# Up-projection of six of twelve hidden chunks in the last two token tiles by Strassen's seven block products

## The chip, the cores and the metric

The kernel runs on one core of a Trainium2 chip. The metric is device time in microseconds of one launch; before the change it is 357.53 us (median of three runs, 356.72 to 358.25). The profiled execution used below took 358.99 us by the same clock, of which its trace covers 357.2 us from the first to the last instruction. Engines are called as in the profile: PE (matrix multiply), PEld (its weight loads), DVE (vector), ACT (scalar), POOL (GpSimd), SP (the queue that issues most transfers).

## The reference

The program is blockwise causal attention followed by a gated feed-forward layer.

```python
scores = scale * np.matmul(q, k.transpose(0, 1, 3, 2))   # (8, 8, 576, 64) per q, k, v; blocks of 64
... masked softmax over scores -> attn ...
x = np.matmul(attn, v).transpose(0, 2, 1, 3).reshape(4608, 512)
gate = np.maximum(x @ w_gate, 0.0)        # w_gate: 512 x 1536
val = x @ w_val                            # w_val:  512 x 1536
out = (gate * val) @ w_out                 # w_out:  1536 x 512
```

Inputs and the output are float32; inside the kernel the matrix products take bf16 and accumulate in float32.

## The kernel before, in words

**Tiles.** The 4608 tokens are handled as nine tiles of 512: tiles j = 0 to 7 hold the first 512 tokens of batch j, tile 8 holds the 64 last tokens of all eight batches. `xT_of(j)` is the transposed attention output of tile j, 128 partitions by four contraction chunks c by 512 tokens; for tile 8 it is `xTt`. The feed-forward of tile j runs while the attention of batch j + 1 runs in between its matmuls, so while tiles 7 and 8 run no attention is left.

**Up-projection.** The 1536 hidden features are twelve chunks f of 128. For every chunk `product` (L866) issues four matmuls of 128 x 512 for the gate and four for the value, one per contraction chunk c. ACT takes the relu of the gate out of the PSUM bank (`relu`, L876) and DVE multiplies it with the value's bank into the hidden tile `hT` (`hidden`, L886). The banks come from the pool `ffnp`, a ring of three; there are also two double banks `sc`, used by the attention, and one bank `one`.

**Down-projection.** From tile 2 on (`SEVEN = 2`) `seven_products` forms the output by Strassen's scheme over the blocks (chunk parity) x (token half) and (chunk parity) x (output half): seven sums of products instead of eight, each of 12 matmuls of 128 x 256 (L789), whose left sides are sums of hidden blocks. The pairs of chunks (2c, 2c + 1) are numbered c = 0 to 5. `Sums.make_part` (L748) makes the left sides on DVE: part 0 for the products 5 and 2, part 1 for product 1, part 2 for the products 6 and 7. The order of the products is 5 into the bank `y` and 2 into the bank `z` (first for c = 0 to 3, then for c = 4, 5), then 1, 3, 4, 6, 7. ACT, DVE and POOL combine the banks in float32 tiles `ob` (a ring of four; L823 to L846), which transfers on the ACT queue then write out; one store is kept back and issued in the next tile.

**Order.** Every engine executes its instructions in the order in which the program issues them. `ffn_gen` is a generator that yields after a few matmuls; the attention's steps carry a place in that sequence of yields (`AT`), and a loop at the end of the kernel issues each step when the generator has come to its place.

Of the kernel before, what the change touches and what calls it, by code (L numbers as in the profile page):

```python
# [10 lines left out]
FP = mybir.dt.float32  # L11
BF = mybir.dt.bfloat16
AX = mybir.AluOpType
# [4 lines left out]
def kernel(  # L18
# [10 lines left out]
    nc = tc.nc  # L29
# [9 lines left out]
    FIRST = 3  # L39
    SEVEN = 2  # L40
    BASE = {0: 0, 1: 512, 3: 896, 2: 1024}
    AW = 1600
# [64 lines left out]
    def new_bf():  # L107
        return [sb.tile([128, 2048], BF, name=n, bufs=2) for n in ("q_bf", "k_bf")]
# [593 lines left out]
    def weight_differences(c, eng):  # L702

        two = wo[c // 2][:, 2 * (c % 2) : 2 * (c % 2) + 2, :]
        for d, n in ((two[:, 0, 256:512], two[:, 1, 256:512]), (two[:, 1, 0:256], two[:, 0, 0:256])):
            eng.tensor_tensor(out=d, in0=d, in1=n, op=AX.subtract)

    class Sums:

# [21 lines left out]

        def make_part(self, q, part, k0, k1):
            h, n = self.quads[q], k1 - k0
# [10 lines left out]
            else:  # L744
                out = self.two[q][:, 1024 + 512 * k0 : 1024 + 512 * k1]
                a, b = h[:, 2 * k0 : 2 * k1, 256:512], h[:, 2 * k0 : 2 * k1, 0:256]
                op, m = AX.subtract, 2 * n
            nc.vector.tensor_tensor(  # L748
                out=out.rearrange("p (c n) -> p c n", c=m), in0=a, in1=b, op=op
# [17 lines left out]
    def seven_products(j, quads, sums):  # L767
# [30 lines left out]
        def half(to, p):  # L798
            return to[:, 256 * p : 256 * p + 256]

        def whole(to, which, new=True, cs=range(6)):
            for p in range(2):
                for c in cs:
                    times(half(to, p), which, p, c, new and (p, c) == (0, 0))
                    if c % 2:
                        yield
# [11 lines left out]
        for to, which in ((y, 5), (z, 2)):  # L818
            yield from whole(to, which, cs=range(4))
        for to, which in ((y, 5), (z, 2)):  # L820
            yield from whole(to, which, new=False, cs=(4, 5))
        g = sb.tile([128, 512], FP, name="ob", bufs=4)
# [10 lines left out]
        nc.gpsimd.tensor_tensor(out=c22, in0=g, in1=c12, op=AX.add)  # L833
        yield from whole(z, 4, new=False)
        c21 = sb.tile([128, 512], FP, name="ob", bufs=4)
        nc.scalar.copy(c21, z)
# [11 lines left out]
        else:  # L848
            for p in range(2):
# [7 lines left out]
                )  # L857
                store_later(0, 0, half(g, p), p, p + 1)

    def ffn_gen():  # L860
        for j in range(B + 1):
            hT = []
# [26 lines left out]

            sums = Sums(quads) if j >= SEVEN else None  # L890

            first = 0
# [139 lines left out]
    with tc.manual_schedule(engines={E.PE, E.DVE, E.Activation, E.Pool, E.SP}):  # L1032
# [465 lines left out]
        for b in range(4, B):  # L1498
# [17 lines left out]
            {f"D{c}": lambda c=c: weight_differences(c, nc.vector) for c in range(6)}  # L1516
        )
        for c in range(6):
            AT[f"W{c}"] = (225, 229, 233, 242, 266, 270)[c]
            AT[f"D{c}"] = 293 + 5 * c  # L1520
# [45 lines left out]
```

## Time and profile before

| what | value |
|---|---|
| median of the runs | 357.53 us |
| profiled execution | 358.99 us, span 357.2 us |
| PE busy | 346.6 us (97% of the span), 3173 matmuls |
| DVE, ACT, POOL busy | 206.2, 180.8, 143.6 us |
| PE busy between 292.9 and 352.7 us (tiles 7 and 8) | all of it |
| from PE's last matmul to the end | 4.5 us |

The profile's numbers are read so: a line of a group gives the program line (L866 is line 866 of the kernel above), the engine, the operation, its output and inputs, and the busy time with the mean duration of one instruction; the chain is the sequence of work, followed back from the last instruction, in which each step released the next; a stage's row gives each engine's busy time in that stretch and the clock that PE was granted (1.00 is full speed).

### The profile page before, as it was taken

What the parts mean: (1) busy time and instruction counts of PE and PEld (TensorE: products, weight loads), DVE (VectorE), ACT (ScalarE), POOL (GpSimd) and SP (SyncE); (2) the same over time, 40 slices, a digit from 0 to 9 for tenths busy, and PEclk for the clock granted to TensorE, in tenths of its full rate; (3) what the DMA queues carried; (4) which work ended last, traced back from release to release, by engine and by line L of the source; (5) the groups of instructions that cost most, each with busy time, mean ns of one, the idle gap of its engine ahead of it and who ended that gap; (6) DMA issues with size and microseconds to landing.
All of it is one profiled execution on the core that took longest, in us unless ns stands there. A gap on an engine that the chain in (4) does not pass through costs nothing.

```text
span 357.2 us, 8061 instructions
## 1 busy us (share of the span) xinstructions
PE 346.6 (97%) x3173; PEld 202.8 (57%) x3173; DVE 206.2 (58%) x519; ACT 180.8 (51%) x286; POOL 143.6 (40%) x187
## 2 busy tenths in 40 slices
PE   6999999999999999999999999999999999999994
PEld 3544555545444458555855576557755684485464
DVE  4654445668536675466647772667366745644661
ACT  5942756687235771566355545555465513322321
POOL 4847655589926901590149203940200020020003
PEclk9899999999999999999999999999999999999999
DMA  8999999999999995899259954999310030003004
GB/s 243 296 356 373 323 228 283 194 133 184 158 153 145 144 160 94 150 147 164 58 139 140 122 114 130 124 142 134 110 46 15 17 112 29 2 11 108 1 0 119
DMA packets 155398, 50.02 MB, mean 140 GB/s; under 512 B 134464, under 2 KB 151744, under 8 KB 155360
## 3 DMA queue, kind: packets, MB, share of 16 engines
q0 software_dynamic: 70528, 8.98, 45.2%
q1 hardware_dynamic: 76432, 31.47, 42.8%
q10 hardware_dynamic: 8400, 9.05, 7.8%
q8 instruction: 25, 0.41, 0.5%
q14 instruction: 13, 0.11, 0.1%
HBM read 37.75 MB, written 9.44 MB: 132 GB/s over the span
## 4 chain that ended last, share of the span: by engine, by line
PE 87%; DMA 4%; ACT 4%; DVE 3%; issue 0%; POOL 0%; POOLq 0%; DVEq 0%
PE ffnp L866 47%; PE ffnp L789 13%; PE one L789 5%; PE ffnp L967 3%; PE sc L451 3%; DMA kTm<-k_bf 3%; PE ffnp L586 2%; PE one L451 2%; DMA xT<-xnat 2%; PE one L586 2%; ACT attnT L456 2%; ACT attnT L415 1%; PE one L866 1%; PE one L1018 1%; PE sc L586 1%; PE ffnp L270 1%
## 5 line engine op out<-in xcount | busy, mean ns | idle before, releaser
L886 DVE TENSOR_TENSOR hT<-gate_sb,ffnp 128x512 bf16<-128x512 bf16 x102 | 69.8, 685 | 68.6 <-PE ffnp L866 44.4
L876 ACT ACTIVATE gate_sb<-ffnp 128x512 bf16<-128x512 f32 x107 | 64.4, 605 | 88.2 <-PE ffnp L866 88.0
L866 PE MATMUL ffnp<-xT,wg 128*128 128x512 bf16 x380 | 103.4, 379 | 0.8 <-DMA xT<-xnat 0.8
L866 PE MATMUL ffnp<-xT,wv 128*128 128x512 bf16 x360 | 99.0, 379 | 0.3 <-DVE hT L886 0.3
L833 POOL TENSOR_TENSOR ob<-ob 128x512 f32<-128x512 f32 x7 | 8.8, 1263 | 143.8 <-ACT ob L830 143.8
L866 PEld LDWEIGHTS <-wv 128*128 128x128 bf16 x432 | 39.6, 98 | 45.5 <-issue 5.1
L866 PEld LDWEIGHTS <-wg 128*128 128x128 bf16 x432 | 40.0, 98 | 43.0 <-issue 2.2
L456 ACT ACTIVATE attnT<-sc 128x1024 bf16<-128x1024 f32 x56 | 57.5, 1042 | 0.0
L789 PEld LDWEIGHTS <-stage 128*128 128x128 bf16 x420 | 40.3, 98 | 6.0
L748 DVE TENSOR_TENSOR stage<-hT 128x512 bf16<-128x512 bf16 (+2 forms) x84 | 38.5, 486 | 0.9
L586 PEld LDWEIGHTS <-attnT 128*128 128x128 bf16 x640 | 26.6, 98 | 12.8 <-DVE attnT L1027 1.1
L789 PE MATMUL ffnp<-stage 128*128 128x256 bf16 x252 | 31.4, 273 | 0.0
L339 POOL DMA_DIRECT2D q_bf<-in_q_dram x20 | 17.9, 908 | 24.5 <-DVE hT L886 19.0
L463 ACT ACTIVATE attnT<-one 128x512 bf16<-128x512 f32 (+1 forms) x28 | 15.0, 536 | 25.2 <-PE ffnp L451 23.5
L339 POOL DMA_DIRECT2D v_bf<-in_v_dram x30 | 24.3, 890 | 0.0
L967 PE MATMUL ffnp<-wo,hT 128*128 128x512 bf16 x96 | 23.7, 379 | 0.0
L451 PEld LDWEIGHTS <-kTm 64*128 64x128 bf16 x384 | 13.1, 94 | 14.7 <-issue 8.7
L339 POOL DMA_DIRECT2D k_bf<-in_k_dram x20 | 17.8, 931 | 0.0
L451 PE MATMUL sc<-qTm,kTm 64*128 64x512 bf16 (+1 forms) x168 | 17.7, 305 | 0.0
L789 PEld LDWEIGHTS <-hT 128*128 128x128 bf16 x168 | 16.4, 98 | 1.9
L841 DVE TENSOR_TENSOR ob<-ffnp,ob 128x512 f32<-128x512 f32 x7 | 4.8, 692 | 21.6 <-POOL ob L833 15.0
L830 ACT COPY ob<-ffnp 128x512 f32<-128x512 f32 x7 | 4.1, 586 | 21.9 <-PE ffnp L789 21.9
(144 smaller groups left out, 464.2 us busy)
## 6 DMA issues: line engine op xcount, KB each, us to landing
out_dram<-ob ACTq DMA_DIRECT2D x32, 256.0 KB, 2.4
stage<-in_moe_w_val_dram SPq DMA_DIRECT2D x6, 512.0 KB, 8.7
stage<-in_moe_w_gate_dram SPq DMA_DIRECT2D x6, 512.0 KB, 8.7
stage<-in_moe_w_out_dram SPq DMA_DIRECT2D x6, 512.0 KB, 10.6
q_bf<-in_q_dram POOLq DMA_DIRECT2D x20, 128.0 KB, 4.5
k_bf<-in_k_dram POOLq DMA_DIRECT2D x20, 128.0 KB, 5.3
v_bf<-in_v_dram POOLq DMA_DIRECT2D x20, 128.0 KB, 5.5
stage<-in_v_dram SPq DMA_DIRECT2D x19, 128.0 KB, 5.4
```

The lines of the kernel that those rows point to most:

```text
L339: ins = nc.gpsimd.dma_start(dst, part_of)
L451: nc.tensor.matmul(o, kTm[b % 2][head_of(hh), c, hp, :], qT, start=True, stop=True)
L456: return lambda: nc.scalar.activation(at[:, :, lo : lo + 512], sc, AF.Exp, scale=scale)
L463: nc.scalar.activation(at[:, hh, 1024 : 1024 + w], third[hh][:, 0:w], AF.Exp, scale=scale)
L586: nc.tensor.matmul(av[:, p, :], at[:, col : col + 128], v_bf[b % 2][:, c, h, :], start=(p == 0), stop=(c == p), skip_group_check=True,)
L748: nc.vector.tensor_tensor(out=out.rearrange("p (c n) -> p c n", c=m), in0=a, in1=b, op=op)
L789: nc.tensor.matmul(to, sums.of(c)[which][:, 128 * p : 128 * p + 128], right, start=first, stop=(c == 5), skip_group_check=True,)
L833: nc.gpsimd.tensor_tensor(out=c22, in0=g, in1=c12, op=AX.add)
L866: nc.tensor.matmul(to, (wg, wv)[t][f // 4][:, c, 128 * (f % 4) : 128 * (f % 4) + 128], x[:, c], start=(c == 0), stop=(c == 3),)
L876: nc.scalar.activation(gate_sb, gate, AF.Relu)
L886: nc.vector.tensor_tensor(out=h, in0=gate_sb, in1=val, op=AX.mult)
L967: nc.tensor.matmul(op, hT[f][:, 128 * s : 128 * (s + 1)], wo[f // 4][:, f % 4, n0:n1], start=(f == 0), stop=(f == 11),)
```

## The change

In tiles 7 and 8 (`j >= B - 1`) the chunks 2 to 7, as the pairs (2, 3), (4, 5) and (6, 7), are computed by Strassen's scheme over the blocks (gate, value) x (contraction half) of the weights and (contraction half) x (token half) of x: per pair seven products of four 128 x 256 matmuls each (`times`) take the place of 16 matmuls of 128 x 512. The weight sums (`up_sum`, 15 of them, on DVE) are issued at places in tiles 5 and 6 and lie in the buffers `q_bf` and `k_bf`; the sums of x blocks (`x_sums`, five per tile, on DVE) are issued at the start of tile 7 for tile 7 and late in tile 7 for tile 8. A pair's banks y and z are `sc` banks; ACT copies them out (or takes the relu), POOL adds M5 and M2, DVE forms the two missing corners and multiplies. `make_part` gets an engine argument; three of its calls per tile (for c = 0, 1) move from DVE to POOL. The remaining chunks 0, 1, 8 to 11 are interleaved between the products. In these tiles `seven_products` takes the pairs c = 0, 1, 2, 4 first and c = 3, 5 after them.

```diff
--- before.py
+++ after.py
@@ -38,6 +38,7 @@
     FIRST = 3
     SEVEN = 2
+    PAIRS = (2, 4, 6)
     BASE = {0: 0, 1: 512, 3: 896, 2: 1024}
     AW = 1600
     TW = 256
@@ -705,6 +706,33 @@
         for d, n in ((two[:, 0, 256:512], two[:, 1, 256:512]), (two[:, 1, 0:256], two[:, 0, 0:256])):
             eng.tensor_tensor(out=d, in0=d, in1=n, op=AX.subtract)
+    ups = {}
+    def up_sum(n, which):
+        if not ups:
+            ups["free"] = [
+                t[:, 512 * i : 512 * i + 512].rearrange("p (c f) -> p c f", c=2)
+                for two in (new_bf(), new_bf())
+                for t in two
+                for i in range(4)
+            ]
+        i, lo = divmod(PAIRS[n], 4)
+        f = slice(128 * lo, 128 * lo + 256)
+        g, u = wg[i], wv[i]
+        a, b, op = {
+            1: (g[:, 0:2, f], u[:, 2:4, f], AX.add),
+            2: (u[:, 0:2, f], u[:, 2:4, f], AX.add),
+            5: (g[:, 0:2, f], g[:, 2:4, f], AX.add),
+            6: (u[:, 0:2, f], g[:, 0:2, f], AX.subtract),
+            7: (g[:, 2:4, f], u[:, 2:4, f], AX.subtract),
+        }[which]
+        t = ups[n, which] = ups["free"].pop(0)
+        nc.vector.tensor_tensor(out=t, in0=a, in1=b, op=op)
     class Sums:
@@ -729,7 +757,7 @@
                 if part < 3:
                     self.make_part(q, part, k0, k1)
-        def make_part(self, q, part, k0, k1):
+        def make_part(self, q, part, k0, k1, eng=None):
             h, n = self.quads[q], k1 - k0
             if part == 0:
                 out = self.two[q][:, 512 * k0 : 512 * k1]
@@ -745,7 +773,7 @@
                 out = self.two[q][:, 1024 + 512 * k0 : 1024 + 512 * k1]
                 a, b = h[:, 2 * k0 : 2 * k1, 256:512], h[:, 2 * k0 : 2 * k1, 0:256]
                 op, m = AX.subtract, 2 * n
-            nc.vector.tensor_tensor(
+            (eng or nc.vector).tensor_tensor(
                 out=out.rearrange("p (c n) -> p c n", c=m), in0=a, in1=b, op=op
             )
@@ -798,6 +826,8 @@
         def half(to, p):
             return to[:, 256 * p : 256 * p + 256]
+        early, last = ((0, 1, 2, 3), (4, 5)) if j < B - 1 else ((0, 1, 2, 4), (3, 5))
         def whole(to, which, new=True, cs=range(6)):
             for p in range(2):
                 for c in cs:
@@ -816,9 +846,9 @@
         y = psum_ffn.tile([128, 512], FP, name="ffnp")
         z = psum_one.tile([128, 512], FP, name="one")
         for to, which in ((y, 5), (z, 2)):
-            yield from whole(to, which, cs=range(4))
+            yield from whole(to, which, cs=early)
         for to, which in ((y, 5), (z, 2)):
-            yield from whole(to, which, new=False, cs=(4, 5))
+            yield from whole(to, which, new=False, cs=last)
         g = sb.tile([128, 512], FP, name="ob", bufs=4)
         nc.scalar.copy(g, y)
         nc.vector.tensor_tensor(out=g, in0=z, in1=g, op=AX.add)
@@ -832,6 +862,8 @@
         c22 = sb.tile([128, 512], FP, name="ob", bufs=4)
         nc.gpsimd.tensor_tensor(out=c22, in0=g, in1=c12, op=AX.add)
         yield from whole(z, 4, new=False)
+        if j == B - 1:
+            x_sums(B, (1, 3, 4, 6, 7))
         c21 = sb.tile([128, 512], FP, name="ob", bufs=4)
         nc.scalar.copy(c21, z)
         store_later(1, 0, c21)
@@ -857,6 +889,39 @@
                 )
                 store_later(0, 0, half(g, p), p, p + 1)
+    xsum = {}
+    def x_part(j, cs, hi):
+        if j == B:
+            return xTt[:, 4 * hi : 4 * hi + 4, cs].rearrange("p b h n -> p h b n")
+        return xT_of(j)[:, cs, 256 * hi : 256 * hi + 256]
+    def x_sums(j, which):
+        lo, hi = slice(0, 2), slice(2, 4)
+        for n in which:
+            if (j, "free") not in xsum or not xsum[j, "free"]:
+                two = sb.tile([128, 4, 2, 128], BF, name="perm", bufs=4)
+                two = two.rearrange("p a b n -> p (a b n)")
+                xsum[j, "free"] = [two[:, 0:512], two[:, 512:1024]]
+            t = xsum[j, n] = xsum[j, "free"].pop(0)
+            a, b, op = {
+                1: (x_part(j, lo, 0), x_part(j, hi, 1), AX.add),
+                3: (x_part(j, lo, 1), x_part(j, hi, 1), AX.subtract),
+                4: (x_part(j, hi, 0), x_part(j, lo, 0), AX.subtract),
+                6: (x_part(j, lo, 0), x_part(j, lo, 1), AX.add),
+                7: (x_part(j, hi, 0), x_part(j, hi, 1), AX.add),
+            }[n]
+            out = (
+                t.rearrange("p (c b n) -> p c b n", c=2, b=4)
+                if j == B
+                else t.rearrange("p (c n) -> p c n", c=2)
+            )
+            nc.vector.tensor_tensor(out=out, in0=a, in1=b, op=op)
     def ffn_gen():
         for j in range(B + 1):
             hT = []
@@ -888,6 +953,133 @@
                 hT.append(h)
             sums = Sums(quads) if j >= SEVEN else None
+            def by_pairs():
+                for _ in range(3):
+                    quads.append(sb.tile([128, 4, 512], BF, name="hT", bufs=3))
+                gates = {}
+                def gate(f):
+                    to = psum_ffn.tile([128, 512], FP, name="ffnp")
+                    for c in range(4):
+                        product(to, 0, c, f)
+                        yield
+                    gates[f] = relu(to)
+                def value(f):
+                    to = psum_ffn.tile([128, 512], FP, name="ffnp")
+                    for c in range(4):
+                        product(to, 1, c, f)
+                        yield
+                    nc.vector.tensor_tensor(
+                        out=quads[f // 4][:, f % 4], in0=gates[f], in1=to, op=AX.mult
+                    )
+                def times(to, n, which, new):
+                    i, lo = divmod(PAIRS[n], 4)
+                    f = slice(128 * lo, 128 * lo + 256)
+                    left = {3: wg[i][:, 0:2, f], 4: wv[i][:, 2:4, f]}.get(which)
+                    left = ups[n, which] if left is None else left
+                    if which in (2, 5):
+                        right = x_part(
+                            j,
+                            slice(0, 2) if which == 2 else slice(2, 4),
+                            int(which == 5),
+                        )
+                    else:
+                        right = xsum[j, which].rearrange("p (c n) -> p c n", c=2)
+                    for k in range(2):
+                        for c in range(2):
+                            nc.tensor.matmul(
+                                to[:, 256 * k : 256 * k + 256],
+                                left[:, c, 128 * k : 128 * k + 128],
+                                right[:, c],
+                                start=new and (k, c) == (0, 0),
+                                stop=(c == 1),
+                                skip_group_check=True,
+                            )
+                        yield
+                def ob():
+                    return sb.tile([128, 512], FP, name="ob", bufs=4)
+                def split(t):
+                    return t.rearrange("p (k n) -> p k n", k=2)
+                def pair(n, first, second, mult):
+                    q, k0 = divmod(PAIRS[n], 4)
+                    h = quads[q][:, k0 : k0 + 2]
+                    y, z = bank("sc"), bank("sc")
+                    low, a, b = ob(), ob(), ob()
+                    yield from times(y, n, 5, True)
+                    nc.scalar.copy(a, y)
+                    yield from times(z, n, 2, True)
+                    nc.scalar.copy(b, z)
+                    nc.gpsimd.tensor_tensor(out=a, in0=a, in1=b, op=AX.add)
+                    yield from first
+                    m1 = bank("one")
+                    yield from times(m1, n, 1, True)
+                    nc.vector.tensor_tensor(out=a, in0=m1, in1=a, op=AX.subtract)
+                    yield from times(y, n, 3, False)
+                    high = relu(y)
+                    yield from times(z, n, 4, False)
+                    nc.scalar.copy(low, z)
+                    yield from second
+                    yield from times(y, n, 6, False)
+                    nc.vector.tensor_tensor(out=b, in0=y, in1=a, op=AX.add)
+                    mult.tensor_tensor(
+                        out=h[:, :, 256:512], in0=split(high), in1=split(b), op=AX.mult
+                    )
+                    yield from times(z, n, 7, False)
+                    nc.vector.tensor_tensor(out=a, in0=z, in1=a, op=AX.add)
+                    nc.vector.scalar_tensor_tensor(
+                        out=h[:, :, 0:256],
+                        in0=split(a),
+                        scalar=0.0,
+                        in1=split(low),
+                        op0=AX.max,
+                        op1=AX.mult,
+                    )
+                v, p = nc.vector, nc.gpsimd
+                while len(sums.two) < 3:
+                    sums.two.append(sb.tile([128, 2048], BF, name="stage", bufs=10))
+                yield from gate(0)
+                if j < B:
+                    x_sums(j, (1, 3, 4))
+                yield from value(0)
+                store.pop()()
+                if j < B:
+                    x_sums(j, (6, 7))
+                yield from pair(0, gate(1), value(1), p)
+                yield from gate(8)
+                sums.make_part(0, 1, 0, 2, p)
+                yield from pair(1, value(8), gate(9), p)
+                sums.make_part(0, 0, 0, 2, p)
+                yield from value(9)
+                for part in range(3):
+                    sums.make_part(1, part, 0, 1)
+                yield from pair(2, gate(10), value(10), v)
+                sums.make_part(0, 2, 0, 2, p)
+                yield from gate(11)
+                sums.make_part(1, 0, 1, 2)
+                for part in range(3):
+                    sums.make_part(2, part, 0, 1)
+                yield from value(11)
+                sums.make_part(2, 0, 1, 2)
+                for part in (1, 2):
+                    sums.make_part(1, part, 1, 2)
+                    sums.make_part(2, part, 1, 2)
+            if j >= B - 1:
+                yield from by_pairs()
+                yield from seven_products(j, quads, sums)
+                continue
             first = 0
             if j < 2:
@@ -1515,6 +1707,10 @@
         acts.update(
             {f"D{c}": lambda c=c: weight_differences(c, nc.vector) for c in range(6)}
         )
+        for i in range(15):
+            n, which = i // 5, (5, 2, 1, 6, 7)[i % 5]
+            acts[f"U{i}"] = lambda n=n, which=which: up_sum(n, which)
+            AT[f"U{i}"] = (720 + 100 + 8 * i, 864 + 16 * (i - 5), 864 + 100 + 8 * (i - 10))[n]
         for c in range(6):
             AT[f"W{c}"] = (225, 229, 233, 242, 266, 270)[c]
             AT[f"D{c}"] = 293 + 5 * c
```

## The prediction

> **What bounds the kernel now.** I read the busy line first, then the chain that ended last, then that chain's rows and the engines' busy time in the stretch that changes. In these fences the first two lines are from the page, the next three are rows of the chain (start, length, engine, tile, line, count), the last is a stage (busy time and count for PE, PEld, DVE, ACT, POOL; granted clock; transfers).
>
> ```profile
> PE 346.6 (97%) x3173; PEld 202.8 (57%) x3173; DVE 206.2 (58%) x519; ACT 180.8 (51%) x286; POOL 143.6 (40%) x187
> ...
> PE 87%; DMA 4%; ACT 4%; DVE 3%; issue 0%; POOL 0%; POOLq 0%; DVEq 0%
> ...
> 292.91 20.72 PE ffnp L866 x96
> 313.63 0.87 PE ffnp L789 x8
> ...
> 320.18 2.62 PE ffnp L789 x24
> ...
> 292.92:313.63 20.71, 20.71 (x98) 9.46 (x97) 12.39 (x21) 7.16 (x12) 0.00 (x0) 1.00 0.08 26
> ```
>
> In tile 7 PE never waits: 96 matmuls of 512 columns take 20.72 us (0.216 each), 24 of 256 columns 2.62 us (0.109 each, so half a column count costs half). Tile 8 repeats this. PE's work is the time here, DVE has 8 us to spare in the up-projection and POOL all of it.
>
> Prices come from the groups by form and from DVE's timeline at the end of tile 7's up-projection:
>
> ```profile
> L886 DVE TENSOR_TENSOR hT<-gate_sb,ffnp 128x512 bf16<-128x512 bf16 x102 | 69.8, 685 | 68.6 <-PE ffnp L866 44.4 <-ACT gate_sb L876 20.9 <-ACT stage L500 1.2
> L748 DVE TENSOR_TENSOR stage<-hT 128x512 bf16<-128x512 bf16 x42 | 17.6, 420 | 0.4
> ...
> L841 DVE TENSOR_TENSOR ob<-ffnp,ob 128x512 f32<-128x512 f32 x7 | 4.8, 692 | 21.6 <-POOL ob L833 15.0 <-PE ffnp L789 6.6
> ...
> L838 POOL TENSOR_TENSOR ob<-ob 128x512 f32<-128x512 f32 x7 | 8.9, 1268 | 1.7 <-DMA out_dram<-ob 1.2
> L695 POOL TENSOR_TENSOR stage<-wo 128x512 bf16<-128x512 bf16 x6 | 7.0, 1164 | 0.0
> L692 POOL TENSOR_TENSOR stage<-wo 128x256 bf16<-128x256 bf16 x6 | 4.3, 724 | 0.1
> ```
>
> ```profile
> 312.01 0.69 DVE L886 TENSOR_TENSOR hT<-gate_sb,ffnp 128x512 bf16<-128x512 bf16 x1 [0.43 <-PE ffnp L866]
> 312.62 0.95 DVE L748 TENSOR_TENSOR stage<-hT 128x512 bf16<-128x512 bf16 x3
> 313.74 0.69 DVE L886 TENSOR_TENSOR hT<-gate_sb,ffnp 128x512 bf16<-128x512 bf16 x1 [0.17 <-PE ffnp L866]
> 314.46 0.96 DVE L748 TENSOR_TENSOR stage<-hT 128x512 bf16<-128x512 bf16 x3
> ```
>
> A 0.69 us DVE instruction lets an independent one start after 0.61 (312.01 to 312.62) and one that needs its result after 0.72 (313.74 to 314.46); a 0.42 one after 0.34 by the same overlap. DVE starts 0.27 after PE's last matmul ended (313.47, the chain's start of L789 as the timeline has it, to 313.74), ACT 0.20.
>
> **What is removed: PE work.** Per pair 16 x 0.216 = 3.45 us become 28 x 0.109 = 3.06 us. Three pairs save 1.19 us per tile, 2.37 us in both, if PE never waits. With t = 0 at the tile's first matmul, PE would run: chunk 0 to 1.73, pair (2, 3) with chunk 1 between its products to 6.51, gate 8, pair (4, 5) to 12.16, value 9, pair (6, 7) from 13.02 to 17.80, chunk 11 to 19.53 (before: 20.72). Then the down-projection takes c = 0, 1, 2 and reaches c = 4 at 19.53 + 3 x 0.109 = 19.86.
>
> **What is added, POOL's queue.** Pair (4, 5): M6 ends at 11.72, DVE adds until 12.68, POOL multiplies 128 x 512. That form (bf16 by float32) is not in the trace: 1.16 to 1.27 by its two pure forms, 1.21 taken, to 13.96. Behind it POOL has `make_part(0, 0)`, 1024 elements: from 0.72 (256) and 1.16 (512) the line gives 2.04; lower end the cast of 1024 elements on POOL, 1.04, upper end twice 1.16. It ends at 16.00, and only then POOL starts pair (6, 7)'s float32 add, 1.27: 17.27. DVE's subtraction from M1, which the banks would allow at 15.47, starts at 17.30.
>
> **What is added, DVE's queue.** From 17.30, in issue order: subtraction 0.61; multiply of chunk 10, 0.61; y + a 0.72 (the next needs it); multiply of the high half 0.61; z + a 0.72; relu-multiply 0.72; part 0 of c = 3, 0.34; part 0 of c = 4, 0.42 to its end. That is 4.75: 22.05. The high-half multiply and the relu-multiply read float32 from SBUF, which no row of DVE shows: I take 0.69 by the nearest row with float32 (L841), the low end is 0.42 (L748, bf16).
>
> **The stall.** PE reaches c = 4 at 19.86 and gets its left side at 22.05 + 0.07 (the release that tile 6 shows below): it waits 2.25 us. This wait is new; what queues behind it is the whole down-projection. Then c = 5's sum costs 0.07 (DVE 22.05 less overlap, through two sums and chunk 11's multiply, to 23.65; PE arrives at 23.65), and z of pair (4, 5) 0.06 behind DVE's z + a of the pair before. Per tile: -1.19 + 2.25 + 0.13 = +1.19; two tiles +2.38. If POOL's lateness were hidden altogether, DVE would begin with chunk 10's multiply at 16.93 + 0.27 = 17.20 and end c = 4's sum at 21.33: a stall of 1.54, +0.48 per tile, +0.96 in all. With both unshown DVE forms at 0.42 as well the stall is 1.00, and the two tiles give -0.1: the low end. The upper ends of POOL's two prices add 0.35 per tile: +3.1.
>
> **Tiles 5 and 6.** 15 weight sums of 0.34 to 0.42 on DVE. Those at the down-projections fall into idle DVE time (0.70 before L824, 3.05 before L841), as do the three at tile 6's start (0.41 to 2.5). Two fall where PE already waits for DVE:
>
> ```profile
> 271.55 0.20 DVE L532 TENSOR_TENSOR xtail<-ffnp,recip 64x64 bf16<-64x64 f32 x1
> ...
> 271.82 0.28 PE L451 MATMUL ffnp<-qTm,kTm 64*128 64x256 bf16 x1
> ```
>
> The score matmul into `ffnp` starts 0.07 after DVE has read that bank, 0.08 after its twin into `one` (271.74; at an unhindered visit both start at 218.50). The sum ahead of it delays DVE by 0.34 less the 0.12 idle there, 0.2; the second, 0.34 less about 0.25 of idle, 0.1: +0.3. Between 0 and 0.8 (both in full). The x sums of tile 7 stand before chunk 0's multiply, whose bank PE needs two chunks later; those for tile 8 lie where DVE idles 3.29 us before L841: nothing, unless that idle is gone, then 5 x 0.34 = 1.7. ACT gets four instructions of about 0.6 per pair for two relus, 3.6 more per tile beside 7.16 busy of 20.7: hidden. Transfers are the same; the store that was held back goes out one chunk earlier.
>
> **Sum.** +2.38 + 0.3 = +2.7 us. The profiled execution would be 358.99 + 2.7 = 361.7; it stands 1.46 above the median, so the median becomes 357.53 + 2.7 = 360.2, rounded up to 360.3.
>
> **Two rows against rules of the skill.** First, POOL and DVE side by side:
>
> ```profile
> 84.36 0.60 DVE L254 COPY qTm<-perm 128x512 bf16<-128x512 bf16 x1
> 84.59 0.92 POOL L692 TENSOR_TENSOR stage<-wo 128x256 bf16<-128x256 bf16 x1
> 85.20 0.69 DVE L886 TENSOR_TENSOR hT<-gate_sb,ffnp 128x512 bf16<-128x512 bf16 x1 [0.23 <-PE ffnp L866]
> 85.47 1.15 POOL L695 TENSOR_TENSOR stage<-wo 128x512 bf16<-128x512 bf16 x1
> ```
>
> Beside a DVE copy out of SBUF the POOL add took 0.92, its other instances 0.66; beside a DVE multiply with one input from PSUM nothing lengthened. DVE instructions with both inputs from SBUF beside POOL are what this change adds, and no row has them. The Trainium skill ("SBUF — State Buffer", Who interferes with whom) says they exclude POOL instructions that read SBUF for a whole instruction; by it the outcome would be the second rival's.
>
> Second, the clock:
>
> ```profile
> 8.00:9.00 1.00, 0.32 (x7) 0.18 (x5) 0.70 (x2) 1.00 (x2) 0.87 (x5) 1.00 1.09 349
> 9.00:10.00 1.00, 0.96 (x9) 0.40 (x6) 0.30 (x2) 0.94 (x2) 1.00 (x3) 0.52 1.18 310
> ```
>
> After a microsecond in which PE was busy 0.32 the clock fell to about half (0.52, 0.50, 0.50, 0.78 in the next four), 1.7 us of PE work lost, though no idle time there was over 0.7 us. The Trainium skill ("TensorE: Matmul & The Clock Gate", Part 1: The HAM clock gate) wants an idle window of about 3.4 us first; by it a stall of 2.25 us costs no clock, and by the row up to 1.7 us each.
>
> **The rivals.**
> - Only DVE's own queue shows, POOL being earlier than I have it: +0.2 to +1.5, 357.7 to 359.0. For it: POOL's 2.04 is extrapolated. Against: two straight rows lead to it.
> - POOL and DVE exclude each other on SBUF: sums and the relu-multiply wait for POOL's 1.2 to 2.0 us instructions and POOL for them. Walking the queues so, the subtraction of pair (6, 7) starts near 20.8 instead of 17.3: up to 3.5 more per tile, with half of it as the low end +4.7 to +9.7, 362 to 367; about 364.5. For it: the 0.92; against: the copy has another form.
> - The clock falls in the stall: +1.7 per tile on the sum, 363.6. For it, the 9 us row; against, a clock of 1.00 through 100 to 105 us, where PE was busy 4.23 of 5.
> - Other side: faster. The left side of c = 4 is ready at PE's arrival because DVE's pair chain is shorter; the point that decides is a stall of 1.06 per tile (1.19 less 0.13). At no stall the change gives -2.37 + 0.3, 355.4. For it: DVE is 40% idle; against: after M7 DVE still has over 3 us to do and PE only 2.06 before c = 4.
>
> **How the numbers follow.** A measurement can tell about 0.5% (1.8 us) from no change, so "same" is 355.7 to 359.3. My forecast (359.3 to 361.5) has 0.37, DVE alone 0.20, exclusion 0.24, the clock 0.06, the faster side 0.13. Faster is the last, 0.13; same is DVE alone, 0.20; slower the rest, 0.67. The range 357.0 to 365.5 leaves out the faster side and the top quarter of the exclusion, 0.19. The forecast's own range is 359.3 to 361.5.
>
> **What would show it.** In the profile after: PE waiting once per tile, about 2.2 us, for a DVE sum (L776) just after tile 7's and tile 8's up-projection, and no other wait over 0.2; POOL's 1024-element sums at 2.0; DVE's subtraction (L1027) of the third pair released by POOL. Wrong if that wait is under 1 us, if POOL or DVE instructions are stretched, or if a stage's clock is under 1.00.

## The result, and the profile after

The change made the kernel slower: 371.43 us (370.44 to 372.64, four runs) against 357.89 us (356.72 to 360.09, four runs), a ratio of 1.037 (95% interval 1.031 to 1.043). Forecast were 360.3 us and a range of 357.0 to 365.5. The profiled execution after took 371.13 us with a span of 369.3 us.

From the page of the kernel after, the busy line and the shares of the chain that ended last:

```profile
PE 346.3 (94%) x3202; PEld 211.4 (57%) x3245; DVE 230.1 (62%) x558; ACT 186.5 (51%) x298; POOL 167.6 (45%) x203
...
PE 81%; DVE 6%; DMA 4%; issue 3%; ACT 2%; SPq 1%; POOL 0%; DVEq 0%; POOLq 0%
```

PE is busy for the same time in a span 12 us longer, and DVE has grown from 3% to 6% of the chain. The chain gives a ruler: the last 24 matmuls of a tile's down-projection (the products M6 and M7, 2.62 us) are a row of their own. First the kernel before for tiles 5 and 6, then the one after for tiles 5 to 8 (start, length, engine, tile, line, count):

```profile
252.90 2.62 PE ffnp L789 x24
...
290.29 2.62 PE ffnp L789 x24
```

```profile
251.62 2.62 PE ffnp L817 x24
...
289.20 2.62 PE ffnp L817 x24
...
325.04 2.62 PE ffnp L817 x24
...
361.90 2.63 PE ffnp L817 x24
```

Tile 6 takes 37.58 us instead of 37.39, that is 0.19 more for the weight sums. (Of the 1.28 us by which this execution is ahead at tile 5, 1.26 were there at tile 2's end, before anything that the change touches.) From there tile 7 takes 35.84 and tile 8 36.86 us, where the kernel before has 29.89 each. Without any wait it would be 29.89 - 1.19 = 28.70. So the tiles lose 7.14 and 8.16 us, and three things hold all of it. The first is two waits per tile, from the waits of PE (engine, tile and line, what it waited for: us in total, times, longest):

```profile
PE ffnp L817 <- DVE stage L776: 5.9, 2, 3.0
PE ffnp L817 <- DVE hT L978: 3.5, 2, 1.7
```

In PE's timeline for tile 7 they stand one after the other (start, length, operation; in brackets the idle time and who ended it):

```profile
310.79 1.03 PE L931 MATMUL ffnp<-xT,wv 128*128 128x512 bf16 x4
313.55 0.49 PE L817 MATMUL ffnp<-wo,stage 128*128 128x256 bf16 x3 [1.73 <-DVE hT L978]
317.00 1.25 PE L817 MATMUL ffnp<-wo,stage 128*128 128x256 bf16 x5 [2.97 <-DVE stage L776]
318.04 1.91 PE L817 MATMUL one<-wo,stage 128*128 128x256 bf16 x8
```

Counted from where the previous matmul should have handed over, PE waits 1.90 us for chunk 10's multiply, which still holds the bank that the down-projection's `y` takes, and then 3.12 us for c = 4's sum: 5.02 per tile, the same in both. The second thing is in the last two rows: from the start of one row to the start of the next, 5 matmuls of 256 columns take 1.04 us and 8 take 1.71, 0.21 each where 0.109 is the price. The stages of one microsecond say why (busy time and count of PE, PEld, DVE, ACT, POOL; then PE's granted clock):

```profile
316.00:317.00 1.00, 0.00 (x0) 0.00 (x1) 0.97 (x4) 0.00 (x0) 0.00 (x0) 1.00 0.00 0
317.00:318.00 1.00, 1.00 (x5) 0.73 (x6) 1.00 (x3) 0.00 (x0) 0.00 (x0) 0.50 0.00 0
318.00:319.00 1.00, 1.00 (x7) 0.71 (x5) 0.96 (x5) 0.00 (x0) 0.00 (x0) 0.50 0.00 0
319.00:320.00 1.00, 1.00 (x7) 0.69 (x6) 0.61 (x2) 0.00 (x0) 0.00 (x0) 0.50 0.00 0
320.00:321.00 1.00, 1.00 (x9) 0.82 (x8) 0.00 (x0) 0.29 (x1) 0.00 (x0) 0.80 0.00 0
321.00:322.00 1.00, 1.00 (x12) 0.90 (x10) 0.67 (x1) 0.30 (x1) 0.00 (x0) 1.00 0.00 0
```

The clock is at half for 3.4 us, and 1.65 us of work is lost in tile 7. In tile 8 it is at half for 6.8 us, of which the first 2 lie in the wait, and 2.31 us are lost. The third thing is small: waits for banks inside the up-projection, 0.47 and 0.82 us. Together 2 x 5.02 + 3.96 + 1.29 = 15.29, less the 2.37 of PE work saved, plus 0.19: 13.1 of the 13.5 us between the medians.

Why DVE is so late shows where its timeline and POOL's are laid side by side (tile 7 begins at 291.65):

```profile
306.42 0.68 DVE L978 TENSOR_TENSOR hT<-gate_sb,ffnp 128x512 bf16<-128x512 bf16 x1
307.02 5.28 DVE L776 TENSOR_TENSOR stage<-hT 128x512 bf16<-128x512 bf16 x3
312.22 0.68 DVE L1027 TENSOR_TENSOR ob<-one,ob 128x512 f32<-128x512 f32 x1
```

```profile
305.90 2.57 POOL L776 TENSOR_TENSOR stage<-hT 128x1024 bf16<-128x1024 bf16 x1
308.44 1.45 POOL L1023 TENSOR_TENSOR ob<-ob 128x512 f32<-128x512 f32 x1
309.84 2.17 POOL L776 TENSOR_TENSOR stage<-hT 128x1024 bf16<-128x1024 bf16 x1
```

Three sums of c = 2, which took 0.95 us before, take 5.28: they end when POOL's three instructions are through. One by one they end near 308.8, 310.0 and 312.3, each 0.1 to 0.3 us after one of POOL's (308.47, 309.89 and 312.01): the two engines take turns, a whole instruction each. The multiply at 306.42, with one input from PSUM, goes through POOL's 2.57 us unhindered. The subtraction of the third pair starts 20.57 us into the tile; the prediction had 17.30, its second rival "near 20.8".

### The profile page after: what moved, and what is told of

It is laid out like the page before. It is cut to its first block, busy times and chain, and to the rows that moved or that the text cites. A ratio compares the mean times of both kernels' runs of the same rounds, so it can differ in the third digit from the quotient of the medians.

```text
span 369.3 us, 8258 instructions
## 1 busy us (share of the span) xinstructions
PE 346.3 (94%) x3202; PEld 211.4 (57%) x3245; DVE 230.1 (62%) x558; ACT 186.5 (51%) x298; POOL 167.6 (45%) x203
## 4 chain that ended last, share of the span: by engine, by line
PE 81%; DVE 6%; DMA 4%; issue 3%; ACT 2%; SPq 1%; POOL 0%; DVEq 0%; POOLq 0%
PE ffnp L931 39%; PE ffnp L817 13%; PE one L817 6%; PE ffnp L1159 5%; PE sc L452 3%; DMA stage<-in_v_dram 3%; DVE stage L776 2%; PE sc L997 2%; PE one L452 2%; PE ffnp L587 2%; PE one L587 2%; PE one L931 1%; DMA qTt<-q_bt 1%; DVE ob L1039 1%; PE sc L587 1%
## 5 line engine op out<-in xcount | busy, mean ns | idle before, releaser
L931 PE MATMUL ffnp<-xT,wg 128*128 128x512 bf16 x340 | 93.8, 379 | 0.9
L941 ACT ACTIVATE gate_sb<-ffnp 128x512 bf16<-128x512 f32 x95 | 57.2, 605 | 71.0 <-PE ffnp L931 70.5
L931 PE MATMUL ffnp<-xT,wv 128*128 128x512 bf16 x315 | 90.1, 379 | 1.5 <-issue 0.6
L951 DVE TENSOR_TENSOR hT<-gate_sb,ffnp 128x512 bf16<-128x512 bf16 x78 | 53.3, 683 | 50.6 <-PE ffnp L931 26.4
L931 PEld LDWEIGHTS <-wv 128*128 128x128 bf16 x384 | 34.9, 98 | 36.8 <-issue 3.6
L931 PEld LDWEIGHTS <-wg 128*128 128x128 bf16 x384 | 35.4, 98 | 35.4 <-issue 2.4
L817 PEld LDWEIGHTS <-stage 128*128 128x128 bf16 x420 | 42.1, 103 | 18.2 <-DVE stage L776 6.5
L776 DVE TENSOR_TENSOR stage<-hT 128x512 bf16<-128x512 bf16 (+2 forms) x84 | 43.6, 556 | 0.7
L587 PEld LDWEIGHTS <-attnT 128*128 128x128 bf16 x640 | 26.6, 98 | 13.5 <-issue 2.0
L1159 PE MATMUL ffnp<-wo,hT 128*128 128x512 bf16 x90 | 22.4, 379 | 0.2
L817 PE MATMUL ffnp<-wo,stage 128*128 128x256 bf16 x84 | 13.7, 302 | 9.4 <-DVE stage L776 5.9
L452 PEld LDWEIGHTS <-kTm 64*128 64x128 bf16 x384 | 13.3, 94 | 15.3 <-issue 9.7
L853 ACT COPY ob<-ffnp 128x512 f32<-128x512 f32 x7 | 4.1, 586 | 26.9 <-PE ffnp L817 20.8
```

The costliest lines, as they stand in the source:

```text
L452: nc.tensor.matmul(o, kTm[b % 2][head_of(hh), c, hp, :], qT, start=True, stop=True)
L587: nc.tensor.matmul(av[:, p, :], at[:, col : col + 128], v_bf[b % 2][:, c, h, :], start=(p == 0), stop=(c == p), skip_group_check=True,)
L776: (eng or nc.vector).tensor_tensor(out=out.rearrange("p (c n) -> p c n", c=m), in0=a, in1=b, op=op)
L817: nc.tensor.matmul(to, sums.of(c)[which][:, 128 * p : 128 * p + 128], right, start=first, stop=(c == 5), skip_group_check=True,)
L931: nc.tensor.matmul(to, (wg, wv)[t][f // 4][:, c, 128 * (f % 4) : 128 * (f % 4) + 128], x[:, c], start=(c == 0), stop=(c == 3),)
L941: nc.scalar.activation(gate_sb, gate, AF.Relu)
```

## The experiments

Two claims were to be tested: that POOL and DVE exclude each other (A), against a POOL or DVE queue that is merely too long (B); and that 4 us of the loss are clock (C). The ruler is the one above: tiles 7 and 8, against 28.70 us without a wait.

| run | time, us (kernel before beside it) | tile 7, us | tile 8, us |
|---|---|---|---|
| the change | 371.43 (357.89) | 35.84 | 36.86 |
| e1, POOL writes zeros | 360.69 (357.69) | 30.87 | 31.22 |
| e2, all sums on DVE | 361.69 (357.69) | 32.97 | 31.42 |
| e3, filled waits, bank taken | 376.15 (357.69) | 39.21 | 37.88 |
| e5, filled waits, bank free | 367.68 (357.88) | 34.28 | 34.61 |
| e6, c = 2 by copies | 371.01 (357.88) | 36.31 | 37.09 |
| e9, c = 2 with a PSUM input | 365.20 (358.36) | 33.41 | 32.16 |
| e4, reordered | 358.23 (357.69) | 29.63 | 29.97 |
| e7, reordered, halves of one tile | 373.64 (357.88) | 37.65 | 38.03 |
| e8, reordered, more banks | 355.87 (357.66) | 28.70 | 28.70 |

**e1: POOL writes zeros and reads nothing.** POOL's three block sums are left out.

```diff
+            if eng is not None:
+                w = out.shape[1] // 2
+                for i in range(2):
+                    eng.memset(out[:, w * i : w * i + w], 0.0)
+                return
```

> The three block sums that POOL makes in tiles 7 and 8 are replaced by POOL writing zeros of about the same total length into the same places; POOL then reads nothing from SBUF there, and the sums themselves are left out (the output is not the reference's). Theory A (a DVE instruction with both inputs in SBUF and a POOL instruction that reads SBUF shut each other out for a whole instruction): DVE's three sums of c = 2 fall from 5.28 to about 0.96 us, the third pair's subtraction starts near 17.6 us after the tile's start instead of 20.57, the wait for chunk 10's multiply is gone, the one for c = 4's sum is 2.0 to 2.3 per tile, and the time is 361 us (360 to 363; 1.5 more at most if the clock still falls). Theory B (POOL's queue is simply too long, or the sums wait for POOL by a semaphore): the times of POOL's work stay, DVE's sums stay near 5 us, and the time stays at 371.

360.69 us. DVE's timeline, POOL's timeline and PE's waits in e1 (tile 7 begins at 291.99):

```profile
307.23 2.01 DVE L781 TENSOR_TENSOR stage<-hT 128x512 bf16<-128x512 bf16 x3
309.16 0.68 DVE L1032 TENSOR_TENSOR ob<-one,ob 128x512 f32<-128x512 f32 x1
```

```profile
306.10 0.98 POOL L779 MEMSET stage<- 128x512 bf16 x2
307.15 1.27 POOL L1028 TENSOR_TENSOR ob<-ob 128x512 f32<-128x512 f32 x1
308.36 0.98 POOL L779 MEMSET stage<- 128x512 bf16 x2
```

```profile
PE ffnp L822 <- DVE stage L781: 3.2, 2, 1.6
```

Two memsets take 0.98 us together where a 1024-element sum took 2.17 to 2.57. So POOL's queue is shorter here too, not about as long as expected, and e1 alone does not settle whether POOL is merely too long; e9 below does. The three sums take 2.01 and not 0.96 while POOL's float32 add, which does read, runs beside the first of them; the memset beside the other two does not hold them up. The subtraction starts at 17.17, and one wait per tile is left, 1.59 us in the profile or 1.75 counted as above. The clock stays at 1.00 in both tiles.

**e2: the sums go to DVE.**

```diff
-                sums.make_part(0, 1, 0, 2, p)
+                sums.make_part(0, 1, 0, 2)
```
(and likewise for parts 0 and 2.)

> The three block sums that POOL makes in tiles 7 and 8 are given to DVE, which gets some 1.7 us more work per tile; nothing else changes. Theory A (exclusion): POOL keeps only its float32 adds and high-half multiplies, DVE no longer meets them except at the relu-multiply, the wait before c = 4 is about 2.9 us per tile and the only long one, and the time is 363 us (362 to 366, the upper end if the clock falls in the wait). Theory B (DVE's own queue is what comes too late): 1.7 us more per tile on DVE make it 374 to 375.

361.69 us: more work for DVE and 9.7 us less time, so a DVE queue that is merely too long does not explain the loss. POOL's queue is emptied here, so its half of B stays open until e9. The waits, and one stage out of each tile's restart:

```profile
PE ffnp L817 <- DVE stage L776: 4.2, 2, 2.1
```

```profile
315.00:316.00 1.00, 1.00 (x7) 0.69 (x6) 1.00 (x5) 0.00 (x0) 0.00 (x0) 0.50 0.00 0
```

```profile
348.00:349.00 1.00, 1.00 (x12) 0.80 (x9) 1.00 (x5) 0.35 (x1) 0.00 (x0) 1.00 0.00 0
```

The wait is shorter than A said (2.1 in the profile, 2.2 counted as above, instead of 2.9), which puts the time just under the interval. The two tiles wait alike, 2.08 us each, yet the clock falls in the first and not in the second, and tile 7 is 1.55 us longer: the price of one fall, within one execution.

**e3 and e5: PE works through the waits.** Both put 8 and 13 matmuls on zeros into the two waits; they differ in the bank written to.

```diff
+    def fill(n):
+        for _ in range(n):
+            nc.tensor.matmul(spare[0], ident, zeros, start=True, stop=True)
...
+                    if j >= B - 1 and to is y and new and (p, c) == (0, 4) and which == 5:
+                        fill(13)
...
                 yield from by_pairs()
+                fill(8)
```

> In tiles 7 and 8, 8 matmuls of 512 columns on zeros (1.73 us) are put ahead of the down-projection's first product and 13 (2.81 us) ahead of c = 4's first product, into an unused half of a PSUM tile, so that PE works where it waited 1.90 and 3.12 us. Theory C (4.0 of the 12.9 us are TensorE clock that falls to 0.50 after the waits): the clock stays at 1.00 in both tiles' down-projections, and the time falls from 371.4 to 367.4 us. Against it (the clock's share was misread): the time stays at 371.4, or rises by what the extra matmuls overhang.

376.15 us, a miss. The unused half of the PSUM tile is not free: the extra matmuls wait for z + a, the last reader of the other half (waits of PE in e3).

```profile
PE sc L799 <- DVE ob L1050: 7.3, 2, 3.7
```

So e3 has a longer wait with 21 matmuls behind it, and tells nothing on the clock's share. It does add that after waits of 3.66 and 3.65 us the clock fell in tile 7 and stayed at 1.00 in tile 8.

> As e3, but the 8 and 13 matmuls on zeros go into the PSUM bank of chunk 11's gate, which ACT has read by the time PE arrives there and which nothing takes before M1; in e3 they stood behind a wait of their own. Theory C (4.0 of the 12.9 us are TensorE clock that falls to 0.50 after the waits of 1.9 and 3.1 us): PE works through both waits, the clock stays at 1.00 in both tiles, and the time is 367.4 us, 4.0 below the kernel after. Against it (the clock falls for another reason, or the low clock was hidden behind DVE anyway): 371.4 or more.

367.68 us, 3.75 below the change. PE's timeline in e5 has the same two waits, filled:

```profile
310.99 1.89 PE L799 MATMUL ffnp<-zeros,ident 128*128 128x512 bf16 x8
312.88 0.49 PE L823 MATMUL ffnp<-wo,stage 128*128 128x256 bf16 x3
313.21 2.97 PE L799 MATMUL ffnp<-zeros,ident 128*128 128x512 bf16 x13
316.34 0.72 PE L823 MATMUL ffnp<-wo,stage 128*128 128x256 bf16 x5 [0.16 <-DVE stage L776]
```

The five matmuls after them take 0.72 us instead of 1.25, at a clock of 1.00. DVE was no earlier; what went is the clock's share alone. C holds.

**e6 and e9: which DVE instructions are shut out.** In e6 the three sums of c = 2 become copies; in e9 they keep their first input and take the second from PSUM.

```diff
+            if one:
+                nc.vector.tensor_copy(out.rearrange("p (c n) -> p c n", c=m), a)
+                return
```

> DVE's three sums of c = 2 in tiles 7 and 8 become copies of their first input, of the same shapes; POOL keeps its three sums and everything else stays (c = 2's left sides are wrong, the output is not the reference's). Theory A (what is shut out is an instruction with two inputs in SBUF): the three copies take about 1.0 us together beside POOL's sum instead of 5.28, POOL's float32 add starts about 1.7 us earlier, the third pair's subtraction starts near 18.1 us after the tile's start instead of 20.57, one wait of 2.6 per tile is left, and the time is 362 us (361 to 365, with the clock). Theory D (any DVE work on SBUF beside POOL's reads is held up): the copies stay at 3 to 5 us together and the time near 371.

```diff
+            if other is not None:
+                w = 512 if part != 1 else 256
+                b = other[:, 0:w].rearrange("p (c n) -> p c n", c=m)
```

> DVE's three sums of c = 2 in tiles 7 and 8 keep their first input and their shapes, and take their second input from chunk 9's value bank in PSUM instead of from SBUF (c = 2's left sides are wrong, the output is not the reference's); POOL keeps its three sums. e6 showed that a copy with one input and its output in SBUF is held up as the sums are, so the question is what frees DVE. Theory A' (DVE shares with POOL a way into SBUF that it uses for a second SBUF input and for copies, and not for one SBUF input beside one from PSUM): the three take about 1.8 us together (0.69 + 0.40 + 0.69) instead of 5.28, the third pair's subtraction starts near 18.1 us after the tile's start instead of 20.57, one wait of 2.6 per tile is left, and the time is 362 us (361 to 365, with the clock). Theory D (any DVE work on SBUF of this kind beside POOL's sum is held up): the three stay at 4.5 us or more and the time near 371.

Neither run forms c = 2's real left sides. DVE's timeline in e6, then in e9, and POOL's in e9:

```profile
306.69 4.97 DVE L777 COPY stage<-hT 128x512 bf16<-128x512 bf16 x3
```

```profile
307.62 1.60 DVE L779 TENSOR_TENSOR stage<-hT,ffnp 128x512 bf16<-128x512 bf16 x3
310.35 0.69 DVE L1033 TENSOR_TENSOR ob<-one,ob 128x512 f32<-128x512 f32 x1 [1.12 <-POOL ob L1029]
```

```profile
306.51 2.57 POOL L779 TENSOR_TENSOR stage<-hT 128x1024 bf16<-128x1024 bf16 x1
309.05 1.27 POOL L1029 TENSOR_TENSOR ob<-ob 128x512 f32<-128x512 f32 x1
310.27 2.13 POOL L779 TENSOR_TENSOR stage<-hT 128x1024 bf16<-128x1024 bf16 x1
```

e6 gave 371.01 us: my wording of A, "two inputs in SBUF", was too narrow, since a bf16 copy from SBUF to SBUF is held up as the sums are (4.97 against 5.28). (Its time equals the change's partly by chance: the first wait is 0.3 us shorter in each tile, 1.41 for 1.73, but the clock is at half for 6.8 us in both.) e9 gave 365.20 us: with one input from PSUM the three take 1.60, beside the same POOL sum of 2.57, and the subtraction starts at 18.10 (expected 18.1), released by POOL's add as the prediction had it. The wait is 2.4, or 2.55 counted as above (expected 2.6), and the clock falls in tile 7 only; the time is 0.2 above the interval. POOL's 1024-element sums are as long as in the change (2.57 and 2.13 for 2.57 and 2.17) and the time is 6.2 us less, so a POOL queue that is merely too long does not explain it either. So SBUF-to-SBUF sums and copies of DVE take turns with POOL's reading instructions, and instructions with one input from PSUM do not. The Trainium skill ("SBUF — State Buffer", Who interferes with whom) says the same of both kinds: the sums take the second read way that POOL uses, the copies both shared ways in their fast mode, and a POOL instruction that only writes does not collide with the sums. e1, e6 and e9 agree.

**e4, e7, e8: can the saving be had?** e4 gives POOL only the float32 adds and the three high-half multiplies, runs gate chunks early, joins sums and makes those of parts 1 and 2 inside the down-projection.

```diff
-                yield from pair(1, value(8), gate(9), p)
-                sums.make_part(0, 0, 0, 2, p)
...
+                yield from pa(0)
...
+                yield from gate(9)
+                yield from pb(0)
+                yield from gate(8)
+                yield from pc(0)
                 yield from value(0)
...
+                sums.make_part(0, 0, 0, 2)
```

> All block sums are made by DVE, with two to four of a kind joined in one instruction; the gate chunks run early and the value chunks late so that POOL's float32 adds and all three high-half multiplies have time; the sums that the down-projection needs last (parts 1 and 2) are made inside it; one more ob buffer, and the relu results of tiles 7 and 8 lie in attention buffers that are no longer used. Theory A walked through the queues: no wait over 0.3 us in either tile, 2.0 us of the saving of 2.4 is left and tile 6 takes 0.2, so 356.1 us (355.3 to 357.5), against 357.9 before. Rival (DVE's load alone is too much, whatever the order): waits of 1 to 2 us per tile stay, 358 to 361.

358.23 us, level with before (ratio 1.0005, 0.998 to 1.003), 2 us more than expected. That lies in the interval of its rival, a DVE that is simply full (358 to 361); e8 below, with all sums still on DVE and no wait, speaks against the rival. The long waits are gone; small ones for z's bank and for the last sums are left, about 0.9 us in tile 7 and 1.3 in tile 8. e7 was to remove them:

```diff
-                    y, z = bank("sc"), bank("sc")
+                    two = psum_sc.tile([128, 2, 512], FP, name="sc")
+                    y, z = two[:, 0, :], two[:, 1, :]
...
-                    nc.vector.tensor_tensor(out=a, in0=z, in1=a, op=AX.add)
+                    nc.vector.tensor_tensor(out=z, in0=z, in1=a, op=AX.add)
```

> e4 changed in three places: z + a is written back into its PSUM bank, so that the relu-multiply has only one input in SBUF and z + a does not wait for the instruction before it that reads a; y and z of a pair lie in the two halves of one PSUM tile, so that the next pair has banks of its own; and the order of chunks and sums is searched again with that. Theory A: the relu-multiply takes 0.69 beside POOL's multiply instead of 0.93, no wait for a PSUM bank is left, the up-projection takes 19.6 instead of 19.9 and 20.2 us, and the time is 356.2 us (355.5 to 357.5), against 358.2 for e4 and 357.7 before. Rival (DVE is simply full in the up-projection and the last sums stay late): 357.5 to 358.5.

373.64 us, a miss, and by the cause of e3: two halves of one tile are waited for as one. PE's waits in e7:

```profile
PE sc L1012 <- ACT ob L1037: 6.0, 6, 1.8
PE sc L1012 <- DVE ob L1058: 5.2, 6, 0.9
PE sc L1012 <- ACT attnT L956: 4.1, 6, 0.7
```

Each of the six pairs has all three: M2 goes into z and waits for the copy out of y, M4 for y's relu, M7 for the sum that reads y. These eighteen waits of 15.3 us, none over 1.8, left the clock at 1.00. e8 closes the attention's PSUM pool before tile 7 and gives y and z a tile each:

```diff
+                if not from_7:
+                    until_7.close()
+                    from_7.append(
+                        ctx.enter_context(
+                            tc.tile_pool(name="psum_yz", bufs=4, space=bass.MemoryType.PSUM)
+                        )
+                    )
...
+                    y, z = (from_7[0].tile([128, 512], FP, name="yz") for _ in "yz")
```

> e4 with four changes: y and z of a pair get PSUM tiles of their own out of four banks (in e7 two halves of one tile, which are waited for as one), z + a is written back into z's bank so that the relu-multiply has one input in SBUF only, the previous tile's last store is issued after the first gate's relu instead of ahead of it on ACT's queue, and the order of chunks and sums is searched again. Theory A: no wait for a PSUM bank, none of DVE's last sums late, the relu-multiply at 0.69 where e4 has 0.93; the up-projection takes 19.6 us in both tiles, and with 0.2 for tile 6 the time is 355.9 us (355.2 to 357.2), against 358.2 for e4 and 357.8 before. Rival (DVE is simply full in the up-projection, so that the last sums stay late whatever the banks): 357.3 to 358.5.

355.87 us (355.07 to 356.62) against 357.66: a ratio of 0.9948 (0.9928 to 0.9967): faster than both kernels, by half a per cent over the one before. The chain in e8 has the ruler at exactly 28.70 us for both tiles:

```profile
289.21 2.62 PE ffnp L819 x24
...
317.91 2.62 PE ffnp L819 x24
...
346.61 2.63 PE ffnp L819 x24
```

The relu-multiply shows the exclusion in small. In e4 it has both inputs in SBUF, in e8 one in PSUM; each runs beside the same POOL multiply (the timeline of e4, POOL and DVE, then that of e8):

```profile
310.64 1.16 POOL L1058 TENSOR_TENSOR hT<-attnT,ob 128x512 bf16<-128x512 bf16 x1 [3.09 <-DVE ob L1057]
...
311.42 0.93 DVE L1063 SCALAR_TENSOR_TENSOR hT<-ob 128x512 bf16<-128x512 f32 x1
```

```profile
309.20 1.16 POOL L1067 TENSOR_TENSOR hT<-attnT,ob 128x512 bf16<-128x512 bf16 x1 [3.18 <-DVE ob L1066]
...
309.76 0.69 DVE L1072 SCALAR_TENSOR_TENSOR hT<-yz,ob 128x512 bf16<-128x512 f32 x1
```

e8 changed order, banks, the tile that z + a is written to and the place of one store together; which of them carries how much of the 2.4 us between e4 and e8 was not separated.

## Why the prediction was wrong

- **PE's saving: right.** 1.19 us per tile was forecast; e8, where nothing waits, has 29.89 - 28.70 = 1.19.
- **The place of the wait: right, its size wrong.** c = 4's sum was forecast to hold PE for 2.25 us; it held it for 3.12. A second wait, 1.90 for chunk 10's multiply and its bank, was not in the walk, because DVE was never late enough in it. The two are one lateness met twice: PE got c = 4's sum 25.35 us into the tile, 3.23 after the forecast's 22.12, and the subtraction was 3.27 late.
- **POOL's queue: the step that failed.** "DVE's subtraction starts at 17.30" came from POOL's and DVE's durations, each as if alone. Alone they were well sized: the multiply 1.16 for 1.21 taken, the 1024-element sum 2.17 for 2.04, the relu-multiply 0.69 for 0.69. But DVE's three sums took 5.28 for 0.96, and the subtraction started at 20.57. So the term that failed is the overlap: POOL's and DVE's instructions were added up as if they could run side by side. Without POOL's block sums (e1) the subtraction starts at 17.17, c = 4's sum reaches PE at 21.96 and the time is 360.69, near the forecast's 17.30, 22.12 and 360.3. With POOL's sums whole and DVE's c = 2 sums not shut out (e9) it is 18.10; the 0.8 that is left is POOL's first sum at 2.57, which starts beside DVE's relu-multiply, and its start at 14.26 instead of 13.96. Of the signs that the prediction named for being wrong, two are in the profile: stretched instructions and a clock under 1.00.
- **The choice between row and rival: wrong.** The prediction showed the row that decides (a POOL add of 0.92 beside a DVE copy; the others took 0.66 to 0.73, not all 0.66) and set it aside because "the copy has another form". e6 shows that a copy and a sum behave alike. The rival had the mechanism, the place (20.8 against 20.57) and a price of up to 9.7 us; the waits and bank stalls less the saving came to 10.04 + 1.29 - 2.37 = 9.0. It was given 0.24. Its low end was added up wrongly: half of 3.5 us per tile on top of +2.7 makes +6.2, not +4.7.
- **The clock: wrong twice.** It was priced at nothing in the forecast, and as a rival it was added to the forecast's own stall instead of to the exclusion's. Stalls of 5 us per tile and a clock that falls in a stall are not alternatives: the one brings the other. The rival's 1.7 per tile was well sized (1.65 and 2.31; 3.75 by e5). With both, its own numbers give up to 357.5 + 9.7 + 3.4 = 370.6; the range ended at 365.5 because the rivals were taken one at a time and the top quarter of the exclusion was left out.
- **Tile 6: right.** +0.19 for +0.3 forecast over tiles 5 and 6; tile 5 took 37.38 us for 37.39.
- **The other side, faster: its point is borne out.** It was to be reached at a stall under 1.06 us per tile. e1 (1.75) is over it and slower than before, e8 (none) under it and faster.

## What to carry to other kernels

Before work is spread over DVE and POOL, list which instructions read SBUF on both: a DVE sum or copy from SBUF to SBUF beside a POOL sum cost up to the length of the POOL instruction here, so a queue walk has to let the two take turns. Giving such work to one engine (e2) was worth 9.7 us, although DVE got more to do. Taking one operand from PSUM was worth 6.2 in e9, a probe that does not form c = 2's sums; e8 uses it where the program allows, by writing z + a back into its bank. Add up rivals that feed each other, above all a stall and the clock that falls in it.

## What was not expected of the hardware

- **The clock's fall comes in steps of 3.4 us, and a wait's length does not decide it.** From the granted clock per microsecond, the half-clock time was 3.4 us after tile 7's wait in the change, in e2, e3 and e9, and 6.8, twice that, in the change's tile 8 and in both tiles of e6. It fell with waits of 2.08 us (e2, tile 7) and 2.38 (e9, tile 7), and not with 2.08 (e2, tile 8), 2.39 (e9, tile 8) or 3.65 (e3, tile 8). The changes lie on a grid: in each trace, the time from one change of the clock to the next is a whole number of steps of 3.413 us, for example 30.72 us, nine steps, at full clock between the half-clock times of tiles 7 and 8 in the change. Here are two windows of that grid in e2, the last before the fall in tile 7 and the one with most of tile 8's equal wait (stages of 3.41 us):

```profile
310.67:314.08 3.41, 1.33 (x11) 0.83 (x10) 3.38 (x9) 0.19 (x1) 0.00 (x0) 1.00 0.00 0
...
344.80:348.21 3.41, 1.69 (x15) 1.39 (x16) 3.38 (x10) 0.00 (x0) 0.00 (x0) 1.00 0.00 0
```

PE was busy 0.39 of the first and 0.50 of the second. In all the traces, from tile 7 on, a full clock fell at the end of every window in which PE was busy 0.39 or less (0.13 and 0.23 in the change, 0.35 in e9) and of none with 0.43 or more (0.43 in e3's tile 8, 0.46 in e9's; e7 never went under 0.48 while it had work). So it matters how much of a wait falls into one window. PE's busy share is not the whole rule: the kernel before fell at 9 us after a window with 0.61. The Trainium skill ("TensorE: Matmul & The Clock Gate", Part 1: The HAM clock gate) has a free-running window of 3.4 us, which fits these lengths and the dependence on the moment; its idle window of about 3.4 us ahead of a fall does not fit the wait of 2.08.

- **Turns are whole instructions.** Three DVE sums, of 0.96 us together, stretched to 5.28 beside POOL instructions of 2.57, 1.45 and 2.17; neither engine lost to the other more than an instruction at a time.
- **A PSUM tile is waited for as a whole.** In e3 and e7 a write to one half waited for readers of the other half. It goes with the tile and not with the bank: in e8, where y and z are tiles of their own, no such wait is left.
